# Weight sums on VectorE, and two stretches of a planned order rewritten, in an attention and MoE kernel

## The chip, the cores and the metric

The kernel runs on one core of a Trainium2 chip. The metric is the device time of one launch in microseconds. TensorE multiplies, VectorE and GpSimd (POOL in the profile) do elementwise work, ScalarE (ACT) activations, and SyncE (SP) issues most DMAs. Each engine works off its own queue in order.

## The reference

```python
def rmsnorm(x, g):
    rms = np.sqrt(np.mean(x * x, axis=-1, keepdims=True) + 1e-06)
    return x / rms * g
q_n, k_n = (rmsnorm(q, g_q), rmsnorm(k, g_k))
scores = scale * np.matmul(q_n, k_n.transpose(0, 1, 3, 2))
attn = softmax(scores)                    # written out in the reference
attn_out = np.matmul(attn, v)             # batch 8, 12 heads, 448 rows, head size 64
x = attn_out.transpose(0, 2, 1, 3).reshape(3584, 768)
h = x @ w_in                              # 768 x 2048
g = h * np.clip(h + 3.0, 0.0, 6.0) / 6.0
out = g @ w_out                           # 2048 x 768
```

## The kernel before

**Attention.** The 48 pairs of heads (6 for each of 8 batches) pass through a pipeline. For a pair, SP loads queries, keys and values (`ld`, line 464). GpSimd or ScalarE squares (`sq`, lines 405 and 403; `sqh` for half of the queries), VectorE reduces (`red`, lines 493 and 527), ScalarE makes the inverse root in two instructions (`ln` and `ex`, lines 469 and 472), and GpSimd scales queries and keys into `qks` (`sc`, or `sch` for half of the queries, line 408). They are transposed on TensorE (`tr`, `trh`) and copied out (`cq`, `ck`, `cqh`), or from the 14th pair on transposed by a DMA on SP's queue (`dt`, line 600), after which the keys are scaled by the gains (`kt`, lines 608 and 610). Then follow scores (`s`, line 633), exponentials on ScalarE (`e`, line 639), the product with the values (`av`, line 719), its normalisation (`rd`, `xn`), and a transpose into `xT` (`dx`). Values are cast by `cv`, on GpSimd, ScalarE or VectorE (lines 387 and 393). The first six pairs are worked on in halves of their queries (lines with `first`).

**Hidden layer.** `h_group` multiplies `xT` with a column block of `w_in` into one of two banks `M` of PSUM (line 817, `h3`). ScalarE makes `ts` from the bank (`relu`, line 770), VectorE multiplies `ts` and the bank into `gT` (`gate`, line 773). Only then is the bank free for the product after the next.

**Output layer.** For two tiles of rows at once the kernel uses a scheme with seven products in place of eight (`y_pair`). It needs sums of columns of `gT` (`gsum`, line 882, 128 x 1024 elements; `ga` in the trace and below) and six sums of blocks of `w_out`, made once in `wsums` into `wb` (line 843, VectorE, 128 x 1536 elements each). Two of the seven products use a block plus its neighbour; for these `wsums` adds one block onto another in place with four DMAs on GpSimd's queue that accumulate (`wa`, line 850), each ordered after all six sums.

**Order.** Nothing is run where it is written. Every piece is a numbered step that `Plan.add` records with the steps it depends on; `Plan.emit` sends the steps out in the order of the list `ORDER`, each on the first of its possible engines unless `WAY` says the second (1) or third (2). The order of the list is also forced on each engine's queue, so a step that waits holds up all behind it on its engine.

The steps named below are:

- 59, 60: root of the first pair's first queries (`ln`, `ex`); 62: their scaling; 66, 67: their transpose and copy; 209: squaring of the first pair's other queries; 68, 69: squaring of the second pair's keys and first queries; 76, 89, 233: scalings of the second pair's keys and of the two halves of the third pair's queries; 102, 104: first scores.
- 756 to 761: the six sums of weight blocks; 762 to 765: the four additions in place.
- 699, 905: gates; 910: the product that refills the bank which 905 empties.
- 914, 915, 922, 923, 932: the five sums of columns of the first tile pair of that block; 916 to 929: four of its seven products (924 reads what 922 writes, 928 what 923 writes).
- 782, 804: exponentials; 784: scaling of transposed keys; 783, 747: DMA transposes.
- 767, 851, 1114, 819, 876: squarings; 799, 825, 883: casts of values.

Of the kernel before, what the change touches and what calls it, by code (L numbers as in the profile page):

```python
# [11 lines left out]
A_ADD = mybir.AluOpType.add  # L12
# [201 lines left out]
def kernel(  # L214
# [11 lines left out]
    nc = tc.nc  # L226
# [156 lines left out]
    plan = Plan()  # L383
# [443 lines left out]
    def wsums():  # L827
# [20 lines left out]
        for o, x, r, w in adds:  # L848
            def f_a(_, o=o, x=x):
                em(nc.gpsimd.dma_start(out=o, in_=x, accum_op=A_ADD))  # L850
            i = plan.add("wa", [POOL], f_a, [r, w], [w])
            plan.ops[i][3].update(ws)
# [305 lines left out]
```

## Time and profile before

| what | value |
|---|---|
| runs shown | 420.34, 510.44, 1018.97 us (median 510.44) |
| the profiled execution's own time | 421.77 us |
| its span, first to last instruction | 420.0 us |
| mean granted TensorE clock | 0.992 |
| TensorE, VectorE, ScalarE, GpSimd busy | 401.7, 293.3, 288.6, 267.3 us |
| DMA | 69.34 MB, mean 165 GB/s |

The three runs lie far apart. The profiled execution is close to the lowest. In a timeline row stand the start and the length in microseconds, the engine, the source line, the operation, what it writes and reads, its size and count, and in brackets how long the engine stood idle before it and what ended that. In a row of the table of stages stand the busy times (with counts) of TensorE, its weight loads, VectorE, ScalarE and GpSimd, then the granted clock, the share of the DMA engines and GB/s. A row of the waits gives the total, the number and the longest. TensorE counts as busy in the warm-up products at the start, which compute nothing that is used.

### The profile page before, as it was taken

The page shows a single profiled execution, that of the slowest core. Times are in us where ns is not written, and L with a number is a line of the kernel's source. Part 1 is how long each engine was busy: PE and PEld are TensorE (multiplying, and loading weights), DVE is VectorE, ACT ScalarE, POOL GpSimd, SP SyncE. Part 2 cuts the span into 40 slices and gives each one's busy share as a digit, 9 for nine tenths or more (in the row PEclk, how much of TensorE's full clock was granted, in tenths as well). Part 3 has the DMA queues.
Part 4 walks back from the last instruction along what each step waited for, and adds up shares of the span by engine and source line. Part 5 has one row for each costly group of instructions (what it writes and reads, how often), then busy time and mean ns, then how long its engine had stood idle before and what let it go on. Part 6 is the DMA issues. An engine that isn't in the chain of part 4 may idle for free. (4 is left out here: it accounts for less than half of the span.)

```text
span 420.0 us, 9957 instructions
## 1 busy us (share of the span) xinstructions
PE 401.7 (96%) x3848; PEld 233.6 (56%) x3848; DVE 293.3 (70%) x546; ACT 288.6 (69%) x529; POOL 267.3 (64%) x244
## 2 busy tenths in 40 slices
PE   7999999989967999999999999999999999999996
PEld 2566787644533555555555555555556555555553
DVE  4998768577897787767857658776566654657683
ACT  5999998878974696978766776957876657232310
POOL 3999788488986576599978949778449161204000
PEclk9999999999996999999999999999999999999999
DMA  7999969999999786895896768835445240302034
GB/s 254 322 288 242 276 126 171 284 277 222 227 209 201 205 196 134 197 232 123 190 206 171 189 138 203 171 101 124 101 115 149 46 97 23 87 0 77 5 103 118
DMA packets 101091, 69.34 MB, mean 165 GB/s; under 512 B 53268, under 2 KB 97588, under 8 KB 101044
## 3 DMA queue, kind: packets, MB, share of 16 engines
q1 hardware_dynamic: 93488, 60.69, 57.6%
q0 software_dynamic: 7360, 7.87, 11.9%
q8 instruction: 30, 0.49, 0.5%
q14 instruction: 17, 0.14, 0.1%
q10 hardware_dynamic: 196, 0.15, 0.1%
HBM read 50.23 MB, written 11.01 MB: 146 GB/s over the span
## 5 line engine op out<-in xcount | busy, mean ns | idle before, releaser
L817 PE MATMUL M<-xT,w_in_sb 128*128 128x448 bf16 x600 | 131.8, 355 | 6.0 <-DVE gT L773 5.6
L639 ACT ACTIVATE eT<-S 112x896 bf16<-112x896 f32 x112 | 100.0, 916 | 6.7 <-PE S L633 6.5
L408 POOL TENSOR_TENSOR qks<-qk,rs 112x512 bf16<-112x512 f32 (+1 forms) x83 | 88.2, 1094 | 24.4 <-ACT rs L472 14.5
L773 DVE SCALAR_TENSOR_TENSOR gT<-ts,M 128x448 bf16<-128x448 f32 x116 | 71.2, 616 | 43.5 <-ACT ts L770 43.0
L770 ACT ACTIVATE ts<-M 128x448 f32<-128x448 f32 x116 | 63.1, 545 | 50.9 <-PE M L817 49.0
L817 PEld LDWEIGHTS <-w_in_sb 128*128 128x128 bf16 x672 | 60.6, 98 | 63.1 <-issue 17.5
L901 PEld LDWEIGHTS <-gT 128*128 128x128 bf16 x584 | 54.7, 98 | 42.7 <-issue 8.7
L405 POOL TENSOR_TENSOR sq<-qk 112x512 f32<-112x512 f32 (+1 forms) x52 | 54.1, 1061 | 23.6 <-DMA qk<-in_q_dram 21.1
L882 POOL TENSOR_TENSOR ga<-gT 128x1024 bf16<-128x1024 bf16 x16 | 34.0, 2126 | 48.0 <-PE M L901 46.4
L882 POOL TENSOR_TENSOR gT<-gT 128x1024 bf16<-128x1024 bf16 x23 | 51.5, 2245 | 17.7 <-DVE ga L882 13.5
L719 PEld LDWEIGHTS <-eT 112*128 112x128 bf16 x1344 | 51.4, 97 | 13.8 <-issue 2.0
L639 ACT ACTIVATE eT<-X 112x896 bf16<-112x896 f32 x56 | 51.4, 918 | 8.4 <-PE X L633 7.8
L719 PE MATMUL X<-va,eT 112*128 112x65 bf16 x1344 | 53.9, 193 | 1.2 <-ACT eT L639 1.2
L493 DVE TENSOR_REDUCE ssq<-sq 112x16 f32<-112x1024 f32 x42 | 50.7, 1212 | 4.5 <-POOL sq L405 4.4
L901 PE MATMUL M<-wb,gT 128*128 128x384 bf16 x264 | 49.9, 332 | 0.2
L901 PE MATMUL M<-w_out_sb,gT 128*128 128x384 bf16 x248 | 46.2, 326 | 0.5 <-DVE y L925 0.5
L925 DVE TENSOR_TENSOR y<-M,y 128x384 f32<-128x384 f32 x42 | 23.3, 555 | 22.5 <-PE M L901 18.1
L633 PE MATMUL S<-T 64*128 64x448 bf16 x224 | 34.9, 357 | 0.8 <-ACT T L608 0.4
L901 PE MATMUL M<-w_out_sb,ga 128*128 128x384 bf16 x168 | 31.6, 326 | 0.0
L738 DVE TENSOR_TENSOR xn<-X,rd 112x512 bf16<-112x512 f32 x42 | 29.0, 690 | 1.2
L389 ACT COPY y<-M 128x384 f32<-128x384 f32 x26 | 12.4, 479 | 23.9 <-PE M L901 20.3
L901 PEld LDWEIGHTS <-ga 128*128 128x128 bf16 x216 | 20.2, 98 | 14.1 <-issue 1.3
(105 smaller groups left out, 479.0 us busy)
## 6 DMA issues: line engine op xcount, KB each, us to landing
qk<-in_k_dram SPq DMA_DIRECT2D x41, 256.0 KB, 4.2
qk<-in_q_dram SPq DMA_DIRECT2D x41, 256.0 KB, 4.4
vf<-in_v_dram SPq DMA_DIRECT2D x37, 256.0 KB, 4.3
w_in_sb<-in_moe_w_in_dram POOLq DMA_DIRECT2D x4, 768.0 KB, 9.7
w_out_sb<-in_moe_w_out_dram POOLq DMA_DIRECT2D x4, 768.0 KB, 10.2
out_dram<-y SPq DMA_DIRECT2D x8, 336.0 KB, 3.5
out_dram<-y SPq DMA_DIRECT2D x8, 288.0 KB, 3.0
out_dram<-y SPq DMA_DIRECT2D x7, 240.0 KB, 3.3
```

Of the source, the lines that this page charges most:

```text
L405: em(nc.gpsimd.tensor_tensor(out=out, in0=in_, in1=in_, op=A_MULT))
L408: em((nc.vector if e == DVE else nc.gpsimd).tensor_tensor(out=out, in0=in_, in1=by.unsqueeze(3).to_broadcast(list(in_.shape)), op=A_MULT))
L493: em(nc.vector.tensor_reduce(out=ssq[:].rearrange("p i n -> p (i n)"), in_=sq[:].rearrange("p i (n d) -> p (i n) d", d=D), axis=AX_X, op=A ...
L633: em(nc.tensor.matmul(out=ps[:, a, 0:S], lhsT=qkT[r, S + t * TP:S + t * TP + 128], rhs=qkT[r, 0:S], start=True, stop=True))
L639: em(nc.scalar.activation(out=eT[:, t, 0:S2].rearrange("p (a s) -> p a s", a=2), in_=ps[0:TP, :, 0:S], func=EXP, bias=0.0, scale=1.0))
L719: em(nc.tensor.matmul(out=X_ps[:, a, i * E1:(i + 1) * E1], lhsT=eT[:, t, c:c + 128], rhs=va[:, a, t, :], start=(t == 0 and i == 0), stop=( ...
L738: em(nc.vector.tensor_tensor(out=xn[:].rearrange("p i a d -> p a i d"), in0=view()[:, :, :, 0:D], in1=rd[:].unsqueeze(3).to_broadcast([TP, ...
L770: em(nc.scalar.activation(out=ts[:], in_=ps()[:, 0:S], func=RELU, bias=0.5, scale=1.0 / 6.0))
L773: em(nc.vector.scalar_tensor_tensor(out=out, in0=shape(ts[:]), scalar=1.0, in1=shape(ps()[:, 0:S]), op0=A_MIN, op1=A_MULT))
L817: em(nc.tensor.matmul(out=ps()[:, 0:S], lhsT=w_in_sb[:, kt, f * 128:(f + 1) * 128], rhs=xT[:, kt, :], start=(kt == 0), stop=(kt == NKT - 1)))
L882: em((nc.vector if e == DVE else nc.gpsimd).tensor_tensor(out=out, in0=rows(*x), in1=rows(*y), op=op))
L901: em(nc.tensor.matmul(out=ps()[:, 0:nc0], lhsT=lhs[f], rhs=rhs[f][:, c0:c0 + nc0], start=(start and f == 0), stop=(f == HF - 1), skip_grou ...
```

## The change

The change has two parts. The four additions in place of `wsums` run on VectorE as ordinary sums, no longer as accumulating DMAs on GpSimd's queue, and each depends only on the readers and writers of the blocks that it touches.

```diff
-        ws, adds = [], []
+        adds = []
...
                 i = plan.add("wb", [DVE], f_w, reads, [("wb", n, j)])
                 plan.ops[i][3].update(free[n, j])
-                ws.append(i)
             adds += [(b12, b11, rl, ("w12", j)), (b21, b22, rh, ("w21", j))]
         for o, x, r, w in adds:
             def f_a(_, o=o, x=x):
-                em(nc.gpsimd.dma_start(out=o, in_=x, accum_op=A_ADD))
-            i = plan.add("wa", [POOL], f_a, [r, w], [w])
-            plan.ops[i][3].update(ws)
+                em(nc.vector.tensor_tensor(out=o, in0=o, in1=x, op=A_ADD))
+            plan.add("wb", [DVE], f_a, [r, w], [w])
```

`ORDER` is rewritten in two stretches, places 0 to 329 (the start) and 600 to 1099 (some 70 to 155 us); each holds the same steps as before, and the rest of the list is unchanged. `WAY` moves 49 steps to another engine, all in these stretches. Those of the first: to GpSimd 63, 84, 90, 128, 152, 227, 252, 477, 483; to ScalarE 67, 160, 208, 220, 229, 247, 334, 386; to VectorE 76, 78, 89, 101, 233, 310, 374. Of the second: to GpSimd 767, 799, 825, 851, 883, 915, 922, 1095, 1114, 1121, 1172, 1327; to ScalarE 547, 659, 748, 819, 842, 876, 930, 1080, 1147; to VectorE 456, 651, 810, 1069.

The queues around the steps that are named, before and after (worked out from the two lists; those that change place or engine matter):

```
ScalarE, start
  before: 53 54 56 57 68 59 60 69 209 71 72 74 83 84 75 227 103 86 95 87 105 ...
  after:  53 54 56 57 59 60 209 68 69 67 71 72 74 75 83 105 95 86 87 103 213 ...
GpSimd, start
  before: 62 211 76 77 94 88 89 229 99 100 146 78 0 126 127 ...
  after:  62 211 84 77 94 88 227 63 99 215 146 100 90 127 126 ...
ScalarE, 86 to 92 us
  before: 806 795 796 784 782 473 804 853 662 ...
  after:  662 795 806 782 473 821 796 784 804 853 ...
VectorE, 106 to 132 us
  before: 695 825 699 894 873 874 703 1064 707 1090 899 900 711 715 760 719 723 915 905 1054 1059 1060 909 883 913 922 ...
  after:  695 764 699 873 874 703 707 760 711 899 900 715 894 719 1090 723 765 905 909 1059 1054 1060 913 763 921 ...
GpSimd, 113 to 137 us
  before: 1067 1068 914 765 1147 1146 764 762 923 1094 763 1093 932 ...
  after:  914 882 1067 1089 1036 857 883 1088 1035 1114 1068 915 922 923 1146 1093 1172 1094 1173 932 ...
SP, 74 to 84 us
  before: 747 612 642 733 641 613 783 ...
  after:  747 642 612 613 579 550 521 641 732 783 ...
```

After these, VectorE runs 762 between the additions 951 and 954 of the output layer.

293 rows, old and new, of tables (ORDER, WAY) are left out of this document.

## The prediction

> **What bounds the kernel now.** I read the page first, then the table of stages in 10 us windows, then the waits of the worst stage, then that stage's instructions engine by engine.
>
> ```profile
> span 420.0 us, 9957 instructions
> PE 401.7 (96%) x3848; PEld 233.6 (56%) x3848; DVE 293.3 (70%) x546; ACT 288.6 (69%) x529; POOL 267.3 (64%) x244
> PEclk9999999999996999999999999999999999999999
> ...
> 120.00:130.00 10.00, 4.42 (x47) 2.44 (x44) 9.96 (x8) 3.21 (x6) 10.00 (x9) 0.86 1.23 195
> 130.00:140.00 10.00, 10.00 (x77) 5.28 (x76) 6.36 (x12) 5.81 (x11) 2.87 (x2) 0.79 1.20 254
> 140.00:150.00 10.00, 10.00 (x88) 5.18 (x88) 8.19 (x16) 8.37 (x16) 7.33 (x9) 1.00 0.48 132
> ...
> PE M L817 <- DVE gT L773: 5.6, 1, 5.6
> ```
>
> TensorE is busy 96% of the span, so time is won only where TensorE stands still or runs slowly. One stage does both: from 120 to 130 us TensorE works 4.42 of 10 us while VectorE and GpSimd are full, and the granted clock (column after POOL) reads 0.86 and then 0.79. The last row names the wait: one matmul of the hidden layer waited 5.6 us for a gate on VectorE. From 140 us on TensorE is full again at clock 1.00, so what is won before that point is kept if the other engines can follow. Here are VectorE, GpSimd and TensorE around it.
>
> ```profile
> 116.09 2.45 DVE L843 TENSOR_TENSOR wb<-w_out_sb 128x1536 bf16<-128x1536 bf16 x1
> 119.63 7.90 DVE L882 TENSOR_TENSOR ga<-gT 128x1024 bf16<-128x1024 bf16 x1
> 127.45 0.61 DVE L773 SCALAR_TENSOR_TENSOR gT<-ts,M 128x448 bf16<-128x448 f32 x1
> 131.66 0.68 DVE L882 TENSOR_TENSOR gT<-gT 128x1024 bf16<-128x1024 bf16 x1
> ...
> 115.59 2.13 POOL L882 TENSOR_TENSOR ga<-gT 128x1024 bf16<-128x1024 bf16 x1
> 118.84 1.33 POOL L850 DMA_DIRECT2D w_out_sb<-w_out_sb  x1 [1.12 <-DVE wb L843]
> 119.70 2.54 POOL L405 TENSOR_TENSOR sq<-qk 112x512 f32<-112x512 f32 x2
> 121.68 3.14 POOL L850 DMA_DIRECT2D w_out_sb<-w_out_sb  x2
> 123.26 3.71 POOL L882 TENSOR_TENSOR gT<-gT 128x1024 bf16<-128x1024 bf16 x1
> ...
> 121.88 0.65 PE L719 MATMUL X<-va,eT 112*128 112x65 bf16 x16
> 128.11 2.40 PE L817 MATMUL M<-xT,w_in_sb 128*128 128x448 bf16 x6 [5.58 <-DVE gT L773]
> 122.50:128.10 5.60, 0.03 (x1) 0.00 (x0) 5.60 (x3) 1.16 (x4) 5.60 (x6) 0.93 1.27 169
> 128.10:130.50 2.40, 2.39 (x8) 0.77 (x9) 2.37 (x6) 0.00 (x0) 2.40 (x3) 0.50 1.26 205
> 130.50:131.60 1.10, 1.10 (x7) 0.21 (x6) 0.61 (x3) 1.05 (x2) 0.23 (x1) 0.50 1.19 242
> 131.60:134.50 2.90, 2.90 (x13) 1.40 (x12) 1.88 (x3) 1.29 (x3) 0.08 (x1) 0.57 1.22 223
> ```
>
> A sum of gated columns (`ga`, step 915) takes 7.90 us on VectorE; the same size took 0.68 at 131.66. So 7.22 us of it are waiting. Its end, 127.53, lies 0.56 after the end (126.97) of GpSimd's sum that began at 123.26: VectorE waited through two squarings, two accumulating copies of `w_out` (`wa`, line 850) and that sum. Gate 905 stood behind it on VectorE, and TensorE's step 910, which needs the bank that 905 empties, behind the gate: 5.58 us. After it the clock was 0.50 for 3.5 us and 0.57 for 2.9 us.
>
> **The change, part by part.**
>
> *The hole.* The change takes all four `wa` off GpSimd and puts 915 and 922 on GpSimd, so no two-input sum of columns stands ahead of gate 905. The wait goes: **-5.58**. The slow clock goes with it: 2.40 x 0.50 + 1.10 x 0.50 + 2.90 x 0.43 = **-3.0**. At full speed that work would have ended 8.6 us sooner.
>
> *Four additions more on VectorE.* The accumulating copies become VectorE sums of the size of the six that exist.
>
> ```profile
> L843 DVE TENSOR_TENSOR wb<-w_out_sb x6: 946/954/2447, 74.0 to 116.1; 128x1536 bf16<-128x1536 bf16 x6
> 119.12 1.30 PE L817 MATMUL M<-xT,w_in_sb 128*128 128x448 bf16 x6 [0.33 <-DMA qk<-in_k_dram]
> ...
> 156.06 2.06 DVE L882 TENSOR_TENSOR gT<-gT 128x1024 bf16<-128x1024 bf16 x1
> 155.44 2.13 POOL L882 TENSOR_TENSOR ga<-gT 128x1024 bf16<-128x1024 bf16 x1 [1.45 <-PE M L901]
> 157.53 1.50 POOL L408 TENSOR_TENSOR qks<-qk,rs 112x512 bf16<-112x512 f32 x1
> ```
>
> Alone such a sum takes 0.95 us; beside GpSimd's `ga` it took 2.45, its end again 0.8 after GpSimd's (115.59 + 2.13 = 117.72). The rows at 156 show the usual case without `wa`: VectorE waits to the end of one GpSimd instruction, then goes ahead of the next, which is longer by the 0.46 that VectorE holds it. Behind each new sum stand gates: 764 stands before gate 699, 765 before 905, 763 and 762 before additions that empty a bank. The 2.45 us sum cost TensorE 0.33 us (the wait of the matmuls at 119.12, which refill the bank of the gate behind that sum; the row's releaser is a DMA, but that had no part in the matmul's operands). The cover is the attention and score matmuls between two uses of a bank. I take 0.33 for each: **+1.3**. The ends are 0 (sums that meet no GpSimd work) and 4 x 2.45 = +9.8 (no cover at all); I stay at the row where both happened together.
>
> [...]
>
> *What GpSimd takes on.* Ahead of 915 GpSimd gets three squarings (767, 851, 1114) and three value copies (799, 825, 883), and gives up two squarings (819, 876). Then it has 915 and 922, where VectorE had them.
>
> ```profile
> L882 POOL TENSOR_TENSOR ga<-gT 128x1024 bf16<-128x1024 bf16 x16 | 34.0, 2126 | 48.0 <-PE M L901 46.4 <-DVE gT L773 1.6
> L405 POOL TENSOR_TENSOR sq<-qk 112x512 f32<-112x512 f32 (+1 forms) x52 | 54.1, 1061 | 23.6 <-DMA qk<-in_q_dram 21.1 <-DVE y L930 1.5 <-ACT eT L639 0.6
> L393 POOL CAST va<-vf 112x512 bf16<-112x512 f32 x14 | 8.5, 613 | 0.2 <-DMA vf<-in_v_dram 0.2
> 135.96 2.77 PE L901 MATMUL M<-w_out_sb,gT 128*128 128x384 bf16 x16
> ```
>
> 3 x 1.06 + 3 x 0.61 - 2 x 1.06 = 2.9 us. GpSimd ended its first `ga` at 117.72, so it reaches 915 at about 120.6, or 123.5 if VectorE's sums hold it 3 x 0.95. Then 915 and 922 take 4.25: done at 124.9 to 127.7. Step 924, which reads what 922 writes, started at 135.96 and moves up 8.6 to 127.4. So GpSimd is hidden in the middle of its bounds and 0.3 late at their end; the next sum, 923, has the same margin. I cost it at **0**; the end is +3 (one more 2.13 sum and one 0.95 hold ahead of 924).
>
> *The rest of places 600 to 1099 of the order.* Kinds and matmul counts stay; one visible pause is touched.
>
> ```profile
> 88.90 0.67 ACT L608 ACTIVATE T<-T,gp_t 128x448 bf16<-128x448 bf16 x1 [1.29 <-DMA T<-qks]
> 89.47 0.90 ACT L639 ACTIVATE eT<-X 112x896 bf16<-112x896 f32 x1
> 90.42 1.14 PE L719 MATMUL X<-va,eT 112*128 112x65 bf16 x32 [1.20 <-ACT eT L639]
> ```
>
> An exponential (782) stood behind a key scaling (784) that waited for a DMA, and TensorE waited 1.20 us for it. The change puts 782 ahead. But the transpose that 784 waits for (783) stands behind eight loads on SP's queue after its predecessor (747) where it stood behind five, and exponential 804 still stands behind 784. I count **0**, with ends -1.2 and +1.3.
>
> *The start.*
>
> ```profile
> 10.00:20.00 10.00, 9.36 (x127) 5.50 (x124) 9.33 (x25) 9.97 (x27) 9.99 (x14) 1.00 1.10 334
> 5.20 0.21 ACT L472 ACTIVATE rs<-rs 112x8 f32<-112x8 f32 x1
> 7.11 0.63 ACT L403 ACTIVATE sq<-qk 112x512 f32<-112x512 f32 x1 [1.70 <-DMA qk<-in_k_dram]
> 7.64 0.19 ACT L469 ACTIVATE rs<-ssq 112x4 f32<-112x4 f32 x1
> 8.15 0.61 POOL L408 TENSOR_TENSOR qks<-qk,rs 112x256 bf16<-112x256 f32 x1 [6.66 <-ACT rs L472]
> 5.44 0.69 DVE L408 TENSOR_TENSOR qks<-qk,rs 112x512 bf16<-112x512 f32 x1
> ```
>
> ScalarE stood 1.70 us at the second pair's squaring, for a DMA, with the first queries' root (59, 60) behind it. Now the root and the squaring 209 go into that pause: 0.2 + 0.2 + 0.4 = **-0.8**, since ScalarE has no other pause to give (9.97 of 10 us busy from 10 to 20). The ends: -1.7 (the whole pause) and +1.5, because the scalings 76, 89 and 233 go to VectorE, 0.69 for a whole one and some 0.4 for each half, and hold GpSimd, full as well (9.99), that long.
>
> **Sum.** The profiled execution took 421.77 (span 420.0 and 1.8 around it). 421.77 - 5.58 - 3.0 + 1.3 + 0 + 0 - 0.8 = **413.7**. The runs shown are 420.34, 510.44 and 1018.97: the median is a disturbed run, and the lowest agrees with the profile, so I reckon from 421.77 and forecast **413.5**. A change of 2% (8.4 us: 413.3) is about what a measurement of this kernel can tell from no change, and the forecast lies on that edge.
>
> **Rivals.**
>
> 1. *The sum takes the place of the hole.* 765 stands on VectorE just ahead of gate 905, where 915 stood, beside a full GpSimd. If it waits as 915 did, the 8.6 comes back: 421.77 + 1.3 - 0.8 = 422.3. For it: the place and the 7.90. Against: away from `wa` no such wait outlasts one GpSimd instruction in the rows shown. Chance 0.08.
> 2. *Slower.* The same waiting at two of the four sums, 765 and 764 (gate 699 behind it): a second hole of 5.58, 427.9. It decides once GpSimd keeps VectorE out for over some 5 us twice, since one return only restores today's time. Chance 0.05.
> 3. *GpSimd becomes the bound.* It reaches 922 and 923 late by the 3 us above, and its later scalings as well: 416.7. For it: 2.9 us more work plus VectorE's holds; against: from 130 to 140 us it is busy 2.87 of 10. Chance 0.22. [...]
> 4. *The new order wins more than the hole:* the 1.20 at 90 us, and the whole 1.70 at the start: 411.6, or 410 if the sums cost nothing. Chance 0.25.
>
> The forecast keeps 0.40. Nearly half of it lies under 413.3, with all of the fourth rival: faster 0.44; within 2% the rest of the forecast and the first and third: 0.51; slower 0.05. The range is 409 to 420: it takes in the free sums below and GpSimd's lateness with the bad ends of start and order (+3, +1.3, +1.5) above, and leaves out the first two rivals and some luck below 409.
>
> **What would show it.** The stage table should have no window near 4.4 of TensorE and no granted clock below 1.00 between 115 and 140. The wait of L817 for L773 of 5.6 us should be gone, no VectorE sum over some 3 us. If GpSimd is the bound, TensorE's L901 waits for GpSimd's `gT` L882 near 127 us. The start is right if GpSimd's first scaling begins near 6 instead of 8.15 and ScalarE's first exponential before 10.3. I am wrong if the sums at 764, 765 or 763 last over 3 us, or if GpSimd's `ga` starts after 124.

## Result and the profile after

The changed kernel took 417.0 us (median of 20 runs, 415.28 to 420.76), the kernel before 420.82 (20 runs, median). The ratio is 0.9916, 95% interval 0.9891 to 0.9941. Medians here and below take in all runs, while ratios and their intervals leave disturbed executions out, so the two can differ. The change is faster, but by 3.8 us where the forecast, 413.5 from 421.77, said 8.3. The profiled execution took 416.34 us.

Its page, then its table of stages (columns as before), then the waits of TensorE from 100 to 140 us:

```profile
span 414.5 us, 9971 instructions
PE 399.9 (96%) x3848; PEld 233.7 (56%) x3848; DVE 289.9 (70%) x532; ACT 289.4 (70%) x530; POOL 276.8 (67%) x250
PEclk9998999999999999999999999999999999999999
```

```profile
10.00:20.00 10.00, 7.31 (x111) 4.67 (x111) 9.23 (x26) 9.38 (x27) 9.76 (x14) 1.00 1.10 351
30.00:40.00 10.00, 9.18 (x135) 6.74 (x135) 6.44 (x18) 7.89 (x18) 8.08 (x11) 0.83 1.16 222
110.00:120.00 10.00, 8.49 (x103) 4.67 (x100) 9.06 (x14) 6.76 (x13) 10.00 (x10) 1.00 0.71 172
120.00:130.00 10.00, 10.00 (x89) 5.24 (x88) 8.09 (x12) 9.34 (x17) 9.25 (x6) 1.00 0.97 215
130.00:140.00 10.00, 9.97 (x111) 5.97 (x110) 8.26 (x15) 8.87 (x19) 9.71 (x9) 1.00 0.86 212
```

```profile
PE M L816 <- DVE gT L772: 1.5, 1, 1.5
```

The stage of the hole is full: TensorE works 10.00 of 10 us from 120 to 130, at clock 1.00, where it worked 4.42 at 0.86. One smaller wait for a gate is new, at 112 us. The clock's low slice has moved to the start (30 to 40 us: 0.83). In the timeline:

```profile
107.97 3.94 DVE L848 TENSOR_TENSOR w_out_sb<-w_out_sb 128x1536 bf16<-128x1536 bf16 x1
111.83 0.61 DVE L772 SCALAR_TENSOR_TENSOR gT<-ts,M 128x448 bf16<-128x448 f32 x1
122.15 0.95 DVE L848 TENSOR_TENSOR w_out_sb<-w_out_sb 128x1536 bf16<-128x1536 bf16 x1
...
107.97 1.04 POOL L407 TENSOR_TENSOR qks<-qk,rs 112x512 bf16<-112x512 f32 x1
108.97 2.12 POOL L879 TENSOR_TENSOR ga<-gT 128x1024 bf16<-128x1024 bf16 x1
122.31 2.78 POOL L879 TENSOR_TENSOR ga<-gT 128x1024 bf16<-128x1024 bf16 x1 [0.67 <-DVE gT L772]
125.17 4.21 POOL L879 TENSOR_TENSOR gT<-gT 128x1024 bf16<-128x1024 bf16 x2
...
112.49 1.30 PE L816 MATMUL M<-xT,w_in_sb 128*128 128x448 bf16 x6 [1.51 <-DVE gT L772]
```

Sum 764 took 3.94 us beside a scaling and a `ga` on GpSimd, and gate 699 behind it came 1.51 us late for TensorE. The prediction had named a sum of over 3 us as a sign of being wrong. 915 runs on GpSimd (122.31), then 922 and 923. The start, with the row of before that it is to be read against in the second fence:

```profile
5.90 0.61 POOL L407 TENSOR_TENSOR qks<-qk,rs 112x256 bf16<-112x256 f32 x1 [4.41 <-ACT rs L471]
8.99 0.90 ACT L660 ACTIVATE eT<-S 112x896 bf16<-112x896 f32 x1
20.03 1.01 POOL L1003 DMA_DIRECT2D w_in_sb<-in_moe_w_in_dram  x1
31.01 0.36 PE L797 MATMUL M<-xT,w_in_sb 128*128 128x224 bf16 x2 [0.70 <-DMA w_in_sb<-in_moe_w_in_dram]
```

```profile
16.69 1.04 POOL L1006 DMA_DIRECT2D w_in_sb<-in_moe_w_in_dram  x1
```

```profile
28.45:31.86 3.41, 2.15 (x33) 1.23 (x34) 2.40 (x9) 2.85 (x6) 3.41 (x5) 1.00 1.13 329
31.86:35.28 3.42, 3.42 (x41) 2.30 (x40) 1.45 (x3) 3.10 (x5) 3.40 (x5) 0.50 1.20 238
```

The first scaling and the first exponential come earlier (5.90 for 8.15, 8.99 for 10.30), but the first load of input weights (step 0) is issued 3.34 us later on GpSimd's queue, TensorE waits 0.70 us for it, and from 31.86 us the clock is 0.50 for 3.41 us.

**The lead** of one trace over another is the start of the same TensorE steps in before, less their start here, as a mean over the 25 places of before's list that follow the named one. For the changed kernel it is +2.29 us at place 75 (11 us), +0.33 at 150, -0.17 at 275, -2.08 at 325, -1.96 at 600, -3.97 at 900, +5.58 at 1100 and +5.43 at the end. So in this pair of executions the start cost 2 us and the middle brought 7.5. The end is the difference of the profiled executions (421.77 - 416.34); the medians lie 0.95 below the one and 0.66 above the other, which leaves 3.8. A lead compares two single executions and carries their scatter: seven traces below that keep the start of before, order and engines alike, lie between -0.03 and -1.78 us at place 325 (35 us).

### The profile page after: what moved, and what is told of

Read it like the earlier page. It is cut to its first block, busy times and chain, and to the rows that moved or that the text cites. A ratio compares the mean times of both kernels' runs of the same rounds, so it can differ in the third digit from the quotient of the medians.

```text
span 414.5 us, 9971 instructions
## 1 busy us (share of the span) xinstructions
PE 399.9 (96%) x3848; PEld 233.7 (56%) x3848; DVE 289.9 (70%) x532; ACT 289.4 (70%) x530; POOL 276.8 (67%) x250
## 4 chain that ended last, share of the span: by engine, by line
PE 50%; DVE 0%; issue 0%
PE M L898 18%; PE M L816 16%; PE X L718 4%; PE S L898 4%; PE S L632 3%; PE S L816 2%; PE X L816 1%; PE X L632 1%; PE X L898 0%; DVE y L922 0%
## 5 line engine op out<-in xcount | busy, mean ns | idle before, releaser
L816 PE MATMUL M<-xT,w_in_sb 128*128 128x448 bf16 x600 | 130.1, 353 | 1.6 <-DVE gT L772 1.5
L407 POOL TENSOR_TENSOR qks<-qk,rs 112x512 bf16<-112x512 f32 (+1 forms) x81 | 84.0, 1050 | 17.0 <-ACT rs L471 8.9
L404 POOL TENSOR_TENSOR sq<-qk 112x512 f32<-112x512 f32 (+1 forms) x56 | 60.1, 1080 | 20.4 <-DMA qk<-in_q_dram 15.9
L879 POOL TENSOR_TENSOR ga<-gT 128x1024 bf16<-128x1024 bf16 x17 | 36.7, 2163 | 47.9 <-PE M L898 45.1
L898 PE MATMUL M<-wb,gT 128*128 128x384 bf16 x264 | 48.7, 326 | 0.4 <-DVE gT L772 0.3
```

The source lines that it names most:

```text
L404: em(nc.gpsimd.tensor_tensor(out=out, in0=in_, in1=in_, op=A_MULT))
L407: em((nc.vector if e == DVE else nc.gpsimd).tensor_tensor(out=out, in0=in_, in1=by.unsqueeze(3).to_broadcast(list(in_.shape)), op=A_MULT))
L816: em(nc.tensor.matmul(out=ps()[:, 0:S], lhsT=w_in_sb[:, kt, f * 128:(f + 1) * 128], rhs=xT[:, kt, :], start=(kt == 0), stop=(kt == NKT - 1)))
L879: em((nc.vector if e == DVE else nc.gpsimd).tensor_tensor(out=out, in0=rows(*x), in1=rows(*y), op=op))
L898: em(nc.tensor.matmul(out=ps()[:, 0:nc0], lhsT=lhs[f], rhs=rhs[f][:, c0:c0 + nc0], start=(start and f == 0), stop=(f == HF - 1), skip_grou ...
```

## Experiments

### The two stretches apart

*Start of before, middle and sums as changed:* `ORDER = before[:330] + after[330:]`, `WAY` by the same cut.

> The order of the start as before, the middle stretch and the sums as changed. Theory A (the two stretches add up: the new start costs 2.05 us, the middle brings 7.6): the median falls by 2 us against the changed kernel, to about 415.0 us, ratio to before 0.986; in the trace the lead over before is zero up to place 600 and about 7.6 us after 140 us. Rival B (the middle gives back what the start saves, since its gain rests on work that stood in another place): about 417.0 us, 0.991.

Measured 416.11 us (415.56 to 416.72), ratio 0.9892 [0.9852, 0.9932]; lead -0.30 at place 600, +6.33 at 1100. The middle alone carries all of the gain; its six runs scatter less than the 20 of the changed kernel. The time lies between theory A (415.0) and rival B (417.0), and the interval takes in both.

*The other way round:* `ORDER = after[:330] + before[330:]`, accumulating DMAs kept.

> The new order of the start alone; the middle and the four accumulating DMAs as before. Theory A: 2.05 us slower than before, about 422.9 us, ratio 1.005. My prediction on record said 0.8 us faster (1.5 slower at worst): about 420.0 us, 0.998. Rival B (the loss at the start is only a lower clock in some runs): no difference, 1.000.

Measured 423.26 us, ratio 1.0013 [0.9971, 1.0056]: not told from no change, and the interval takes in all three forecasts. The lead is -0.89 at place 600. Three of its twelve runs lie between 417.9 and 419.0 us and eight between 422.7 and 425.3; the profiled execution (417.91 us) is the lowest of all, and its trace shows why a run can be that low. VectorE, GpSimd and TensorE in it:

```profile
120.26 0.69 DVE L882 TENSOR_TENSOR ga<-gT 128x1024 bf16<-128x1024 bf16 x1
...
120.75 2.11 POOL L405 TENSOR_TENSOR sq<-qk 112x512 f32<-112x512 f32 x2
...
134.75 2.43 PE L817 MATMUL M<-xT,w_in_sb 128*128 128x448 bf16 x12 [3.00 <-ACT y L389]
```

Nothing in this stage was changed, yet 915 took 0.69 us and not 7.90: here the squaring on GpSimd began 0.49 us after 915, in before 0.07 (119.70 and 119.63). Another wait then showed, 3.00 us for a copy on ScalarE. Even so this trace gained 4.91 us on before between places 900 and 1100 (lead -0.61, then +4.30), with order, engines and DMAs of that stretch as before. The hole of 5.58 us is thus one outcome of that stretch and not a fixed cost of it.

### What the hole was made of

*Sums on VectorE, order and engines as before:*

> Order and engines as before, only the four additions in place are sums on VectorE. Theory D (the two accumulating DMAs on GpSimd's queue are what stretched step 915 to 7.90 us): 915 takes at most 3 us, the hole of 5.58 us shrinks to under 1.5, and 4 us or more are gained: 416.5 us or less, ratio 0.990. Rival S (squarings and the sum on GpSimd starve 915 in the same way): 915 takes 4.5 us or more, a hole of about 3 us is left, and the four sums of about 1 us each stand on VectorE besides: 418.5 to 421 us, 0.995 to 1.001.

Measured 420.43 us, ratio 0.9997 [0.9964, 1.0029]. VectorE and GpSimd:

```profile
120.33 4.28 DVE L880 TENSOR_TENSOR ga<-gT 128x1024 bf16<-128x1024 bf16 x1
...
119.94 2.04 POOL L405 TENSOR_TENSOR sq<-qk 112x512 f32<-112x512 f32 x2 [1.52 <-DMA qk<-in_k_dram]
121.94 2.13 POOL L880 TENSOR_TENSOR gT<-gT 128x1024 bf16<-128x1024 bf16 x1
```

Without any accumulating DMA 915 still got no turn until two squarings and a sum were through, TensorE waited 3.7 us for the gate, and the clock was 0.50 for 6.83 us again. Theory D falls, and the time is as rival S said. The DMAs can have made 915 longer (7.90 with them, 4.28 without, one trace each), but it does not need them.

*Only 915 to GpSimd, all else as before:*

```diff
-    ..., 883: 2, 915: 1, 922: 1, ...
+    ..., 883: 2, 922: 1, ...
```

> The kernel before with one entry changed: the sum of columns 915 runs on GpSimd, behind 914 and ahead of the squarings 1147 and 1146; everything else, the accumulating DMAs too, as before. Theory S (a sum on VectorE whose GpSimd neighbours follow one another without a gap gets no turn: 7.90 us in the profile of before, 4.28 without the DMAs, 0.69 where it started 0.5 us ahead of the squaring): without it on VectorE the hole on TensorE and the clock of 0.5 are gone, and most of what the new middle brings comes from this one entry: 416 to 417 us, ratio 0.989 to 0.992. Rival R (the new order of the middle is needed, since 922 or a sum of weights on VectorE meets the same neighbours next): a hole of 2 us or more appears later and the time stays above 419.5 us, ratio 0.997 or more.

Measured 416.09 us (413.98 to 419.31), ratio 0.9880 [0.9835, 0.9924], lead +5.92 at place 1100: theory S. One entry gives the median of the whole new middle, though with 5 us between its runs. The late load of the experiment after next did not show in its profile: the squaring 1326 ran on ScalarE at 128.62 us.

*The same with the sums on VectorE* (the edit above and the one before it together):

> Order as before, the sums on VectorE and 915 on GpSimd: the only two edits of the middle that are not order. If the accumulating DMAs do no harm once 915 is away from VectorE: 416.1 us as with 915 alone, ratio 0.988. If the DMAs lengthen GpSimd's work (the sum 923 took 3.71 us beside them, 2.12 alone) and that is on the path: 415 us, 0.985. If the sums on VectorE cost more than the DMAs did: 417 us or more.

Measured 421.05 us, ratio 1.0029 [1.0000, 1.0059]: the third outcome, and the gain of that one entry is lost.

```profile
124.80 5.12 DVE L849 TENSOR_TENSOR w_out_sb<-w_out_sb 128x1536 bf16<-128x1536 bf16 x2
...
131.12 1.44 PE L899 MATMUL M<-wb,gT 128*128 128x384 bf16 x4 [4.51 <-DVE gT L773]
```

Now 764 waits out the second squaring and the sum 923, and 762 a scaling behind them; the two take 5.12 us together, and a gate behind them is 4.51 us late. In the order of before the sums on VectorE thus bring their own hole.

*Squarings 1146 and 1147 to ScalarE, otherwise before:*

> The kernel before; only the two squarings 1146 and 1147, which GpSimd ran beside 915, go to ScalarE. 915 stays on VectorE, the DMAs on GpSimd's queue. [...] Rival D2 (the DMAs that accumulate, still beside it, hold 915 by themselves): 915 takes 4 us or more, 419 us or more.

Measured 421.86 us, ratio 1.0054 [1.0019, 1.0088]. 915 took 0.69 us, although two of the accumulating DMAs were issued beside it, so rival D2 falls. But the time did not fall, it rose a little. TensorE and ScalarE, the table of stages, and the queues' issues from 112 to 138 us (KB each, median us to landing):

```profile
135.59 4.04 PE L817 MATMUL M<-xT,w_in_sb 128*128 128x448 bf16 x12 [5.30 <-ACT y L389]
...
134.54 0.63 ACT L403 ACTIVATE sq<-qk 112x512 f32<-112x512 f32 x1 [6.48 <-DMA qk<-in_q_dram]
```

```profile
120.00:130.00 10.00, 9.45 (x94) 5.67 (x93) 8.46 (x15) 8.07 (x15) 9.40 (x7) 1.00 1.46 145
```

```profile
w_out_sb<-w_out_sb POOLq DMA_DIRECT2D x4, 384.0 KB, 13.5
qk<-in_q_dram SPq DMA_DIRECT2D x4, 256.0 KB, 12.6
```

The changed kernel in the same window, then (from 118 to 138 us) the two runs above with 915 on GpSimd, with the accumulating DMAs and with sums in their place:

```profile
qk<-in_q_dram SPq DMA_DIRECT2D x4, 256.0 KB, 3.5
```

```profile
qk<-in_q_dram SPq DMA_DIRECT2D x3, 256.0 KB, 6.8
```

```profile
qk<-in_q_dram SPq DMA_DIRECT2D x3, 256.0 KB, 4.3
```

This is the second wait. The copy 926 that empties a bank stands on ScalarE behind a squaring (1326) whose query load was in flight together with the accumulating DMAs. With them a query load takes 12.6 us here, in the changed kernel 3.5; the column of the DMA engines' share reads 1.46 in this stage while only 145 GB/s are moved (0.97 and 215 in the changed kernel). Pairs of runs that differ in the DMAs alone agree: 6.8 and 4.3 us in the two rows above, and 9.3 in before against 4.3 with the sums alone. In before, TensorE came to that place so late, after the hole, that it no longer waited (10.00 of 10 us from 130 to 140).

*915 back on VectorE in the changed kernel:* `915: 1`.

> The changed kernel with 915 put back on VectorE, at the same place of the list; 922 stays on GpSimd and waits for it. Theory S: in the new order GpSimd has nothing queued that could run beside 915 for long (922 overwrites what 915 reads), so it takes at most 1.7 us, in the 0.8 us that VectorE stood idle there; the time stays at 416 to 417.5 us. Rival M (the move of 915 to GpSimd is what brings the gain, wherever its neighbours stand): 915 takes 4 us or more, the gate 905 is late by 3 us or more, and 419 to 421 us result.

Measured 417.30 us, ratio 0.9900 [0.9862, 0.9939]. VectorE and GpSimd:

```profile
123.32 0.68 DVE L879 TENSOR_TENSOR ga<-gT 128x1024 bf16<-128x1024 bf16 x1
...
124.08 4.21 POOL L879 TENSOR_TENSOR gT<-gT 128x1024 bf16<-128x1024 bf16 x2 [3.52 <-DVE ga L879]
```

915 took 0.68 us, as theory S said. Its engine matters little where GpSimd's next instruction depends on it (922 overwrites what 915 reads) and so cannot run beside it; the six later traces with this arrangement have 0.68 or 0.69 as well. Rival M falls.

### The sum ahead of gate 699

*Start of before, new middle, 764 moved behind 762:*

> The order of the start as before, the middle as changed, and the sum 764 (3.94 us on VectorE ahead of gate 699, TensorE waited 1.51 us for that gate) moved behind 762, where VectorE stands idle for 0.96 us and the products that need it come 46 places later. If the wait of 1.51 us was on the path: gone, and 1.5 us less than with the start of before and the middle alone (416.11): 414.6 us, ratio 0.985. If another wait takes its place (the gates near 107 us have slack for GpSimd's work, not TensorE): 416 us.

Measured 415.35 us (414.44 to 415.81), ratio 0.9848 [0.9813, 0.9883]. The time lies between the two forecasts. The wait of 1.51 us went, and another came:

```profile
119.20 3.67 DVE L848 TENSOR_TENSOR w_out_sb<-w_out_sb 128x1536 bf16<-128x1536 bf16 x1
...
123.46 1.30 PE L816 MATMUL M<-xT,w_in_sb 128*128 128x448 bf16 x6 [1.22 <-DVE gT L772]
```

Sum 765 now stood beside a scaling and 915 on GpSimd. *The same with 915 on VectorE:*

> The run of 415.35 us (start as before, new middle, 764 behind 762) with 915 on VectorE again, as in the experiment where it took 0.68 us there. Theory S: GpSimd then has nothing to run from 120 us until 915 is through, so the sum 765, which took 3.67 us beside GpSimd's squarings and 915, takes 2 us or less and 915 0.7; the wait that it caused is gone: 414.3 us, ratio 0.982. Rival: 765 and 915 meet GpSimd again and another wait takes the place: 415.4 us or more.

Measured 413.67 us (413.30 to 415.18), ratio 0.9858 [0.9811, 0.9904].

```profile
118.42 1.57 DVE L848 TENSOR_TENSOR w_out_sb<-w_out_sb 128x1536 bf16<-128x1536 bf16 x1
120.69 0.68 DVE L879 TENSOR_TENSOR ga<-gT 128x1024 bf16<-128x1024 bf16 x1
...
121.45 4.21 POOL L879 TENSOR_TENSOR gT<-gT 128x1024 bf16<-128x1024 bf16 x2 [2.28 <-DVE ga L879]
```

```profile
120.00:130.00 10.00, 10.00 (x116) 6.14 (x112) 9.27 (x13) 8.97 (x16) 8.55 (x6) 1.00 1.06 240
```

Sum 765 waits at most for one scaling, 915 for nothing, and no gate is late: theory S. This version has the lowest median of all. By its ratio it is 6.0 us faster than before; its interval overlaps that of the changed kernel and those of several versions below, so that it is the best of them is not shown.

### The start

*Step 0 ahead of 127 in the changed kernel; then also 102 and 103 forward and 764 behind 762; then, from the changed kernel, seven more warm-up products in TensorE's gaps:*

> The changed kernel with one step elsewhere: the first load of input weights (step 0) is issued ahead of 127 and 126 on GpSimd's queue, at about 16.6 us as before, not at 20.0 us. Theory L (the late weights hold up step 267 at 31.0 us, and with it what follows): the load lands near 25 us, the wait of 0.70 us and the clock of 0.5 from 31.9 to 35.3 us are gone, and 1.5 to 2 us come back: about 415.2 us, ratio 0.987. Rival T (TensorE has too little to do from 10 to 20 us whatever the load does, 7.31 us of work where there were 9.36, and the clock falls for that): no change, 417.0 us, 0.991.

> The changed kernel with 764 behind 762 as in the run beside it, the weight load 0 ahead of 127, and at the start the scores 102 right behind 104 on TensorE and their exponential 103 right behind 105 on ScalarE (in the changed kernel 102 stands behind transpose 81, which waits for a scaling on GpSimd, so that the second exponential begins at 10.87 us, 1 us after the first ended at 9.89). Theory Q (that place in TensorE's queue is what eats the 2.3 us that the new start leads by at 11 us): 103 begins at 9.9 to 10.0 us, a lead of about 1 us over the start of before is left at 35 us, and the time is 1 to 1.5 us below the run with the start of before: 413.3 us, ratio 0.982. Rival P (ScalarE, GpSimd and VectorE are all full from 10 to 30 us, 9.4, 9.8 and 9.2 us of 10, so a lead at 11 us cannot last): the lead at 35 us is zero or negative, 414.5 to 416 us.

> The changed kernel; at the start the warm-up products (which compute nothing that is used) are placed in TensorE's gaps from 9.7 to 14.7 us: step 46 as two behind transpose 79, step 47 as five behind scores 102 (gap of 1.14 us), step 49 as two ahead of 110 and step 50 as two. [...] Rival O (the new start is slower by its order, whatever the clock does): 417 us or more, with runs as high as 420.

Measured 417.76 (0.9923 [0.9889, 0.9958]), 417.97 (0.9945 [0.9901, 0.9989]) and 418.38 us (0.9957 [0.9922, 0.9992]): none better than the changed kernel. In the first no wait for the weights is left, but its trace shows the clock at 0.50 from 13.0 to 16.4 us instead. In the second the two first exponentials follow each other (9.43 and 10.22 us) and the lead at 11 us is 2.00, but at 35 us it is -1.36: theory Q falls. In the third TensorE was filled, and sum 764 waited again:

```profile
10.00:20.00 10.00, 9.13 (x119) 5.13 (x116) 9.13 (x24) 9.90 (x28) 9.52 (x13) 1.00 1.10 351
```

```profile
107.23 4.42 DVE L848 TENSOR_TENSOR w_out_sb<-w_out_sb 128x1536 bf16<-128x1536 bf16 x1
...
112.23 1.06 PE L816 MATMUL M<-xT,w_in_sb 128*128 128x448 bf16 x4 [1.99 <-DVE gT L772]
```

The scatter stayed at 415.0 to 421.7 and the time did not fall (418.38 for 417.0), as rival O had said; 4 of 12 runs have a mean clock below 0.995, of the changed kernel 8 of 20, which is too few to tell apart. Its profile shows the clock at 0.50 behind 764's wait (from 112.9 to 116.3 us). The first and the third run still carried that sum. The start was therefore tried again under the middle of the 413.67 us run, where no such wait is left. New and old start were joined at a place of the list: the first 75 or 150 places of one, then what remains in the order of the other.

> The run of 413.67 us with the whole start in the new order. If the two stretches add up and the new start costs what the pairs of runs so far show (0.9 to 2.6 us): 414.6 to 416.3 us. If the new start is harmless and its losses came with the sum 764 alone: 413.7 us.

> The same, with only the first 75 places of the new start (to about 11 us: root and scaling of the first queries, 67, 76 and 84 on other engines), and the rest of the start in the order of before. Theory F (the head is good: it led by 2.3 us at 11 us; the loss comes from what follows): 413 us or less. Theory G (the loss begins in the head, which takes the first scores of the other half first and leaves TensorE without work from 10 to 13 us): as the run with the whole new start, 415 us or more.

> The same, the other way round: the first 75 places as before, the rest of the start in the new order. Theory F: 415 us or more. Theory G: 413.7 us.

> The same, with the first 150 places of the new start (to about 17 us) and the rest of the start as before. If the loss lies from 11 to 17 us (on ScalarE, GpSimd and VectorE, which are full there): as the whole new start. If it lies behind 17 us (the weight load at 20 us, the transposes that follow it): as the first 75 places alone.

> The run of 416.22 us (whole new start, middle of the best run), with the weight load 0 issued ahead of 127, near 17 us in place of 20.3. Theory L (the wait of 1.26 us at 31.8 us and the drop of the clock behind it, 2.1 us of lead together, come from the load): no wait for weights, the lead at 35 us goes from -2.86 to about -0.8 us, and the time is 414.2 to 415 us. Theory O (the order behind place 150 is slower anyway, the load moves the loss about): 415.5 us or more, the lead -1.3 or worse.

| start | median us (range) | ratio to before | lead at 35 us |
|---|---|---|---|
| all old (413.67 us run) | 413.67 (413.30 to 415.18) | 0.9858 [0.9811, 0.9904] | -0.03 |
| all new | 416.22 (415.01 to 418.83) | 0.9881 [0.9843, 0.9919] | -2.86 |
| new up to 75 | 415.32 (413.33 to 416.58) | 0.9853 [0.9818, 0.9888] | -0.43 |
| new from 75 on | 416.01 (415.25 to 419.19) | 0.9886 [0.9851, 0.9922] | -1.28 |
| new up to 150 | 414.45 (413.72 to 415.44) | 0.9839 [0.9810, 0.9867] | -0.25 |
| all new, step 0 ahead of 127 | 414.52 (414.03 to 415.83) | 0.9838 [0.9793, 0.9883] | -0.69 |

The intervals overlap, and the leads are of one trace each, with the scatter named above, so neither column settles the order of these starts. Theory F fails with the first 75 places (415.32, not 413) and theory G with the rest (416.01, not 413.7). The traces do show what happens to the late load. All new, GpSimd and TensorE, then the stage:

```profile
20.28 1.02 POOL L1003 DMA_DIRECT2D w_in_sb<-in_moe_w_in_dram  x1
...
31.83 0.36 PE L797 MATMUL M<-xT,w_in_sb 128*128 128x224 bf16 x2 [1.26 <-DMA w_in_sb<-in_moe_w_in_dram]
```

```profile
30.00:40.00 10.00, 8.61 (x126) 6.00 (x123) 5.86 (x15) 7.38 (x15) 7.85 (x10) 0.83 1.13 219
```

And with step 0 earlier, where no wait for weights is left:

```profile
16.79 1.01 POOL L1003 DMA_DIRECT2D w_in_sb<-in_moe_w_in_dram  x1
```

```profile
30.00:40.00 10.00, 9.47 (x152) 7.04 (x153) 8.38 (x25) 9.70 (x22) 9.61 (x13) 1.00 1.12 217
```

Time and lead of this run (414.52 and -0.69) are what theory L gave. But the same late load stands in six traces, and in only three of them does TensorE wait for it (0.70, 0.76 and 1.26 us). In the other three it finds the weights there. The row of the start alone names no idle time:

```profile
31.13 0.37 PE L798 MATMUL M<-xT,w_in_sb 128*128 128x224 bf16 x2
```

So the wait for the weights is a cost of some executions, and in two of the three the clock fell behind it. How much of the medians it makes is not shown. Under the middle of the 413.67 us run the move of the load went with 416.22 and then 414.52 us, with overlapping intervals, and in the changed kernel it brought nothing (417.76 for 417.0). The lead between 19 and 36 us does not tell either: the traces with the wait lose 1.06 to 2.94 us of it, and those with the start of before, where no such wait stands, 0.46 to 2.37.

What every trace shows is that the early lead does not last. With the new first 75 places it is 1.0 to 2.3 us at 11 us and at most 0.6 at place 100 (14 us); ScalarE, GpSimd and VectorE are full there (9.38, 9.76 and 9.23 of 10 us from 10 to 20 us in the changed kernel). What the rest of the start loses, I did not take apart.

## Why the prediction was wrong

Two terms of the sum failed. The forecast came down by 8.08 us (421.77 to 413.7), the medians by 3.82. The middle with the sums was to bring -5.58 - 3.0 + 1.3 = -7.28 and brought -4.74 by the medians (420.85 to 416.11). The start was to bring -0.8 and brought +0.89 (416.11 to 417.0). That is 2.54 and 1.69 of the 4.26 us that are missing.

- **The hole, -5.58: the first step that failed.** I took the whole wait out of one execution as if every run had it. By the interval of its ratio the middle is worth 2.9 to 6.2 us, less than 7.28. In the profiled pair the size is right: the lead grew by 7.54 from place 600 to 1100. But in the run of the start alone the hole was absent, though that stretch was untouched (915 took 0.69 us, and 4.91 us were gained there), and the profile I reckoned from was a long one: its 421.77 lies 0.95 above the median of before. I had taken it as the base because the lowest of three runs lay near it.
- **The clock, -3.0: nearly right for the middle.** The mean granted clock is 0.9916 in the runs of before that were taken beside the middle alone, and 0.9980 in those of the middle alone. One minus the clock, times the span, gives 3.5 and 0.8 us lost, an estimate: 2.7 us of clock regained. Of the 4.5 us between the mean times of these runs that leaves 1.8 for the wait less the sums, where I had 5.58 - 1.3 = 4.28.
- **What the hole rests on: only half seen.** 915 was kept out by GpSimd's chain, with or without DMAs (4.28 us without). Behind it lay the late query load (3.00 and 5.30 us of TensorE when 915 was free), which I had not seen, and sums on VectorE in the old order wait in their turn (5.12 us). The sums alone (420.43 us), the sums with 915 moved (421.05) and the squarings taken away (421.86) brought nothing; the move of 915 alone did (416.09).
- **The start, -0.8: the second step that failed.** ScalarE's pause was used, and both signs I had named came (first scaling at 5.90, first exponential at 8.99), but of a lead of 1.0 to 2.3 us at 11 us at most 0.6 is left at 14 us, where three other engines are full. No trace with the whole new start has a lead at 35 us. I also left step 0 out of the working, though the listed queue of GpSimd shows it gone from its place behind 78 (it stands five places later); in three of six traces TensorE then waits 0.70 to 1.26 us for that load. Three pairs of versions that differ in the start alone have ratios 0.0013, 0.0024 and 0.0023 higher with the new start, 0.5 to 1.0 us, each within its interval, and in two of the three the mean clock is lower with it (0.994 for 0.998, 0.996 for 0.998). The forecast gain does not show; the size and the cause of the loss stay open.
- **Sums, +1.3: about right in total, by another path.** Sums 765 and 762 cost no wait, 763 took 2.42 us without one, and 764 alone cost 1.51, some five times my 0.33. In another trace (seven more warm-up products) the clock fell to 0.50 behind its wait of 1.99 us. My argument against the first rival, that away from the DMAs no such wait outlasts one GpSimd instruction, fell with 3.94 and 4.28 us.
- **GpSimd, 0, and the rest of the order, 0: right.** 915 began at 122.31, before my limit of 124, and no product waited for a sum of columns. The wait of 1.20 us near 90 us went and was given back at once (lead -0.53 at place 700, -1.37 at 725).
- That the version with the old start, 764 out of the way and 915 on VectorE took 413.67 us, next to my 413.5, is luck: by its ratio it gains 6.0 us, not 8.3.

What decides here are the VectorE sums that outlasted more than one GpSimd instruction: 764 with 3.94 us in the changed kernel (two) and 915 with 7.90 in before (five). A 915 that began 0.49 us ahead of the squaring took 0.69.

## What to carry to other kernels

Before crediting a hole to the wait that the trace names, ask whether every execution has it, and what arrives late behind it: here three waits lay in one place, and most cures of one or two of them bought nothing, since the next one showed. In an order written out by hand, ask of every DMA issue that is moved past others whether its data will be waited for, however small the instruction. A two-input VectorE sum belongs where GpSimd's next instruction depends on it, since a dependency holds GpSimd still (915 took 0.68 or 0.69 us in all seven traces with that arrangement) and luck does not (0.69 or 7.90 in the queues of before).

## What the runs showed of the hardware

- Of 647 two-input VectorE sums of these sizes in all 19 traces, 405 took within 0.1 us of their time alone (0.68 or 0.95), 232 up to 2.2 us more, and 10 more than that, up to 7.90. All ten are the steps 915, 764 and 765, beside GpSimd instructions that followed one another. At which of their boundaries VectorE gets its turn, the traces did not settle.
- Half a microsecond can decide it: the same 915 in the same queues of that stage took 7.90 us where the squaring began 0.07 us after it, and 0.69 where it began 0.49 after it (one trace each). The kernel before ran anywhere from 415.7 to 425.6 us in these runs.
- Within the work the clock fell to 0.50 for 3.41 us or twice that (6.83 in the profile of before, 127.3 to 134.1). Ahead of the drop shown above TensorE was busy 2.15 of 3.41 us. But such a share alone does not bring a drop: in the trace of the start alone a stretch as long with 1.85 us of work was followed by clock 1.00 (first two rows), and a start that left TensorE 6.41 of 10 us (the second of the start's first three runs, last row) went through at 1.00 too:

```profile
129.91:133.32 3.41, 1.85 (x24) 1.24 (x23) 3.38 (x8) 0.00 (x0) 3.41 (x3) 1.00 1.21 232
133.32:136.73 3.41, 1.98 (x11) 1.06 (x11) 0.46 (x2) 1.80 (x7) 0.12 (x1) 1.00 1.58 193
...
10.00:20.00 10.00, 6.41 (x97) 3.76 (x96) 9.12 (x22) 9.01 (x27) 9.60 (x13) 1.00 1.10 350
```

- Beside four accumulating DMAs of 384 KB a 256 KB query load took longer from issue to landing (medians): 9.3 us with them in before and 4.3 with sums in their place, 6.8 and 4.3 with 915 on GpSimd. The longest of these medians was 12.6 us, with the squarings on ScalarE.
